# Turning the first half of h at an item's end, ahead of a run-time branch (sparse attention and expert MLP, one core)

## The chip, the core and the metric

The kernel runs on one core of one Trainium2 chip. The metric is device time in microseconds of the execution: the median of 3 runs.

## The reference

Local and global attention over 8 batches of 8 heads (512 local and 32 global positions, head size 64), and then a mixture of experts on the 4352 rows of 512 values that come out. Only the second part matters here:

```python
xn = x / (np.linalg.norm(x, axis=-1, keepdims=True) + 1e-06)
logits = xn @ en.T / tau
expert_idx = np.argmax(logits, axis=1)
for e in range(E):
    mask = expert_idx == e
    h = np.maximum(x[mask] @ w1[e], 0.0)
    out[mask] = gate_w[mask, None] * (h @ w2[e])
```

There are 8 experts; `w1[e]` is 512 x 1024 and `w2[e]` is 1024 x 512. How many rows an expert gets is known only at run time.

## The kernel before

The attention part writes its rows, sorted by expert, to a table in DRAM (`xs`). Then the expert part works in items of 128 rows of one expert. The number of items depends on the data: it lies between `NSURE` = 32 and `NI` = 48. Items 0 to 31 (`NSURE` - 1) are written out without a branch. Behind them stands a nest of run-time branches (`rest`, L1465): ahead of each further item every engine compares the item count with the item's number and either falls through into the next item or jumps to a closing block (`close`, L1424) that stands far behind. With the inputs here there are 36 items, 0 to 35: four branches fall through, and the fifth is taken.

Numbers are kept in two parts. A tensor is rounded to a high part by a ScalarE cast (`xH`, `hH`, `WH`), and VectorE subtracts that from the tensor to get the low part (`xL`, `hL`, `WL`). A product is then three TensorE products: high by high, high by low, low by high.

An item `w` does two steps, one item apart:

- up, for its own rows: `h = relu(x @ w1)`, in two halves of 512 columns. `up(0)` and `up(1)` are 12 products each. `send_h` (L1332) takes the relu on ScalarE and sends the half of h to DRAM (`hd`) from ScalarE's DMA queue; `get_h` (L1264) brings it back turned by blocks (`hq`) through SP's queue.
- down, for the item before (`pend`): `down(0)` and `down(1)` are 12 products each, 8 with `hH` and 4 with `hL`. Each needs its half of h to be turned on VectorE in blocks of 32 (`turn_h`, L1267, into `hk`) and rounded on ScalarE and VectorE (`split_h`, L1270). There is one `hk`, which both halves use in turn.

Beside this each item turns and splits the rows of the next item (`turn_x` into `xk`, `split_x`), and splits one staged half of an expert's weights, in eight chunks per item (`w_parts`, L1294: cast `WH` on ScalarE, subtraction `WL` on VectorE). An item's result is scaled and scattered by token two items later (`give`, L172: ScalarE `ob`, VectorE the token copy, POOL the scatter).

The order is written out by hand (`tc.manual_schedule()`): each engine runs its instructions in the order in which the code of `item` issues them, and waits by semaphores on the others. TensorE runs `up(0)`, `up(1)`, `down(0)`, `down(1)`. VectorE and ScalarE run, from item 3 on, the order of the last `else` of `item` (L1389 to L1409): turn of x, turn of the first half of h, split of x, one weight chunk, split of that half, turn of the second half, the first relu, and so on, and at the end the five last weight chunks. At an item's start each engine reads its entries of the item table into registers (`entry`, L1212): 

```python
        return eng.value_load(tab["tab"][w : w + 1, i : i + 1], min_val=0, max_val=top)
```

The closing block for item 35 is: turn and split of the first half, the result of item 34, `down(0)`, turn and split of the second half, `down(1)`, the result of item 35.

Of the kernel before, what the change touches and what calls it, by code (L numbers as in the profile page):

```python
# [98 lines left out]
def _sure_items(nt):  # L99
    return (nt - EARLY * P) // P  # L100
# [7 lines left out]
def tile_kernel(ctx: ExitStack, tc: tile.TileContext, qk, va, emb, tau, wraw, cst, out):  # L108
# [5 lines left out]
    NSURE = _sure_items(NT)  # L114
# [30 lines left out]
    def cols(st, lo, hi):  # L145

        r = lo // WRUN
        return st[:, r, lo - r * WRUN : hi - r * WRUN]
# [17 lines left out]
    def turn_blocks(xT, x):  # L166

        nc.vector.transpose(  # L168
            xT.rearrange("p (k t n) -> p t k n", k=4, t=4), x.rearrange("p (t k n) -> p t k n", t=4, k=4)
        )  # L170

    def give(gt, g2, ob):  # L172

        nc.scalar.activation(ob[:, :DM], g2, AF.Copy, scale=gt[:, 0:1])
        nc.vector.tensor_copy(ob[:, DM : DM + 1].bitcast(U32), gt[:, 1:2].bitcast(U32))
        nc.gpsimd.indirect_dma_start(  # L176
            out=out[:, :],
            out_offset=bass.IndirectOffsetOnAxis(ap=ob[:, DM : DM + 1].bitcast(U32), axis=0),
            in_=ob[:, :DM],
            in_offset=None,  # L180
            bounds_check=NT - 1,
            oob_is_err=False,
        )
# [1028 lines left out]
    def entry(eng, i, w, top):  # L1212

        if w < 2:
            return (EARLY * P + w * P, 2 + w, 0, 2 + w)[i]
        return eng.value_load(tab["tab"][w : w + 1, i : i + 1], min_val=0, max_val=top)

    def load_x(w):
        r = entry(nc.sync, 0, w, NE * CAP)
        return rows_of(xrs[w % 2], gts[w % 5], xs[ds(r, P), :], True)  # L1220
# [14 lines left out]
    def parts_of(tH, tL, x):  # L1235
        nc.scalar.copy(tH, x)  # L1236
        nc.vector.tensor_tensor(tL, x, tH, ALU.subtract)

    def flat(t):
        return t.rearrange("p c n -> p (c n)")  # L1240
# [12 lines left out]
    def relu(nh, g):  # L1253
        nc.scalar.activation(  # L1254
            hs[nh].rearrange("p (g k n) -> p k g n", g=4, k=4),
            g.rearrange("p (k g n) -> p k g n", k=4, g=4),
            AF.Relu,
        )

    def put_h(w, nh):  # L1260
        hd = hds[w % 2][nh].rearrange("p n -> (p n)").rearrange("(g p n) -> p g n", g=4, p=P)
        nc.scalar.dma_start(hd, hs[nh].rearrange("p (g n) -> p g n", g=4))

    def get_h(w, nh):  # L1264
        nc.sync.dma_start(hqs[nh], hds[w % 2][nh])

    def turn_h(nh):  # L1267
        turn_blocks(hk, hqs[nh])

    def split_h(nh):  # L1270
        ks = slice(4 * nh, 4 * nh + 4)
        parts_of(flat(hH[:, ks, :]), flat(hL[:, ks, :]), hk)

    def entries(w):
        return entry(nc.scalar, 3, w, 3), entry(nc.vector, 3, w, 3)

    def item(w, pend):

        xH, xL = xHs[w % 2], xLs[w % 2]
        rp = entry(nc.tensor, 2, w, 1)  # L1280
        regs = entries(w)
        if w < 2:
            held.append((w, regs))
        reads = []
        made = []
        todo = [(w, regs, c) for c in range(8)]
        if w == 0:
            todo = todo[:4]
        elif w == 1:
            todo = [(*held[0], c) for c in range(4, 8)] + [(*held[1], c) for c in range(4)]  # L1290
        elif w == 2:
            todo = [(*held[1], c) for c in range(4, 8)] + todo

        def w_parts(n):  # L1294
            for _ in range(min(n, len(todo))):
                v, (ra, rv), c = todo.pop(0)
                cs = slice(c * 512, (c + 1) * 512)
                s3 = cols(st0[v % 2], cs.start, cs.stop).unsqueeze(1)
                a = nc.scalar.copy(WH[c][:, ds(ra, 1)], s3)  # L1299
                b = nc.vector.tensor_tensor(WL[c][:, ds(rv, 1)], s3, WH[c][:, ds(rv, 1)], ALU.subtract)  # L1300
                made.extend([(v, c, a), (v, c, b)])

        def product(o, a, W, hf, start=False, stop=False):
            w3 = W[:, ds(rp, 1), hf * 512 : (hf + 1) * 512]
            return nc.tensor.matmul(o.unsqueeze(1), a, w3, start=start, stop=stop)  # L1305

        def up(nh):
            g = ps_1.tile([P, 512], F32, name="g1")
            for k in range(4):
                c = 2 * k + nh  # L1310
                reads.append(product(g, xH[:, k, :], WH2[c], 0, start=k == 0))
                reads.append(product(g, xH[:, k, :], WL2[c], 0))
                reads.append(product(g, xL[:, k, :], WH2[c], 0, stop=k == 3))
            return g

        out = {}

        def down(nh):
            if nh == 0:
                out["g2"] = g2s[w % 2]  # L1320
            g, ks, made = out["g2"], range(4 * nh, 4 * nh + 4), []
            for k in ks:
                made.append(product(g, hH[:, k, :], WH2[k], 1, start=k == 0))
                made.append(product(g, hH[:, k, :], WL2[k], 1))
            for k in ks:
                made.append(product(g, hL[:, k, :], WH2[k], 1, stop=k == 7))
            return made

        def done():
            give(gts[w % 5], out["g2"], obp.tile([P, DM + 1], F32, name="ob"))  # L1330

        def send_h(nh, g):  # L1332
            relu(nh, g)
            put_h(w, nh)

        ga = up(0)
        if "done" in pend:
            pend["done"]()
        if w > 2 and w + 1 < NI:
            load_w(w + 1)  # L1340
        if w + 2 < NI:
            load_x(w + 2)
        if w == 0:
            send_h(0, ga)
            w_parts(2)
            send_h(1, up(1))
            get_h(w, 0)
            first_w(1, 0, 1)
            get_h(w, 1)
            first_w(1, 1, 4)  # L1350
            w_parts(2)
        elif w == 1:
            w_parts(2)
            send_h(0, ga)
            w_parts(2)
            turn_h(0)
            split_h(0)
            gb = up(1)
            reads.extend(pend["down"](0))
            send_h(1, gb)  # L1360
            get_h(w, 0)
            load_w(w + 1)
            turn_h(1)
            split_h(1)
            turn_x(w + 1)
            split_x(w + 1)
            w_parts(4)
            get_h(w, 1)
            reads.extend(pend["down"](1))
        elif w == 2:  # L1370
            turn_x(w + 1)
            turn_h(0)
            split_x(w + 1)
            split_h(0)
            turn_h(1)
            send_h(0, ga)
            w_parts(2)
            split_h(1)
            gb = up(1)
            reads.extend(pend["down"](0))  # L1380
            send_h(1, gb)
            w_parts(2)
            get_h(w, 0)
            load_w(w + 1)
            w_parts(8)
            get_h(w, 1)
            reads.extend(pend["down"](1))
        else:
            if w < NI - 1:  # L1389
                turn_x(w + 1)  # L1390
            turn_h(0)
            if w < NI - 1:
                split_x(w + 1)
            w_parts(1)
            split_h(0)
            turn_h(1)
            send_h(0, ga)
            w_parts(1)
            split_h(1)
            w_parts(1)  # L1400
            gb = up(1)
            reads.extend(pend["down"](0))
            send_h(1, gb)
            get_h(w, 0)
            w_parts(8)
            get_h(w, 1)
            if w in (8, NSURE - 1):
                nc.gpsimd.drain()
            reads.extend(pend["down"](1))  # L1409
        for v, c, m in made:  # L1410
            for r in reads:
                tc.declare_no_dep(m.ins, r.ins, reason="the other slot")
                tc.declare_no_dep(r.ins, m.ins, reason="the other slot")
        for i, (v, c, m) in enumerate(made):
            for u, d, o in last_made + made[:i]:
                if c == d and (v - u) % 2:
                    tc.declare_no_dep(m.ins, o.ins, reason="another half")
        last_made[:] = made
        after = {"down": down, "next": done}
        if "next" in pend:  # L1420
            after["done"] = pend["next"]
        return after

    def close(pend):  # L1424
        turn_h(0)
        split_h(0)
        if "done" in pend:
            pend["done"]()
        pend["down"](0)
        turn_h(1)  # L1430
        split_h(1)
        pend["down"](1)
        pend["next"]()
# [123 lines left out]
```

## Time and profile before

| what | us |
|---|---|
| median of 3 runs | 693.06 |
| lowest and highest | 692.15, 702.01 |
| profiled execution | 689.4 |
| its span, first to last instruction | 687.5 |
| TensorE busy in the span | 627.8 (91%) |
| VectorE busy | 525.4 (76%) |
| ScalarE busy | 455.0 (66%) |

The profiled execution is one execution; its span leaves out the start and the end around the instructions.  The trace names engines PE (TensorE matmul), PEld (TensorE weight load), DVE (VectorE), ACT (ScalarE), POOL (GpSimd) and SP (SyncE); a "q" behind the name is the engine's sequencer, which handles register work, branches, semaphores and DMA issues, and L1300 is line 1300 of the kernel above. In brackets stands how long the engine was idle before an instruction and what ended that.

### The profile page before, as it was taken

The page shows a single profiled execution, that of the slowest core. Times are in us where ns is not written, and L with a number is a line of the kernel's source. Part 1 is how long each engine was busy: PE and PEld are TensorE (multiplying, and loading weights), DVE is VectorE, ACT ScalarE, POOL GpSimd, SP SyncE. Part 2 cuts the span into 40 slices and gives each one's busy share as a digit, 9 for nine tenths or more (in the row PEclk, how much of TensorE's full clock was granted, in tenths as well). Part 3 has the DMA queues.
Part 4 walks back from the last instruction along what each step waited for, and adds up shares of the span by engine and source line. Part 5 has one row for each costly group of instructions (what it writes and reads, how often), then busy time and mean ns, then how long its engine had stood idle before and what let it go on. Part 6 is the DMA issues. An engine that isn't in the chain of part 4 may idle for free.

```text
span 687.5 us, 23125 instructions
## 1 busy us (share of the span) xinstructions
PE 627.8 (91%) x7425; PEld 492.7 (72%) x7425; DVE 525.4 (76%) x1724; ACT 455.0 (66%) x962; POOL 94.9 (14%) x172
## 2 busy tenths in 40 slices
PE   9889788878888899779999999999999999999994
PEld 4667567666666546648888888888888877878873
DVE  2869777698887877668888888786888877878971
ACT  4777667657676436557777676766677766767761
POOL 2011221212313330001101001010101100110101
PEclk9999999999999999999999999999999999999997
DMA  9998889788898558767654586778877787876550
GB/s 276 321 274 265 253 260 278 211 272 284 280 329 274 158 167 243 245 206 233 192 161 145 150 261 207 202 211 287 239 229 220 222 256 231 229 227 171 147 158 23
DMA packets 125654, 154.66 MB, mean 225 GB/s; under 512 B 15945, under 2 KB 81609, under 8 KB 125528
## 3 DMA queue, kind: packets, MB, share of 16 engines
q1 hardware_dynamic: 81752, 116.32, 57.6%
q10 hardware_dynamic: 38016, 18.88, 9.2%
q0 software_dynamic: 5760, 17.87, 6.9%
q8 instruction: 69, 1.13, 0.7%
q14 instruction: 57, 0.47, 0.2%
HBM read 161.36 MB, written 40.94 MB: 294 GB/s over the span
## 4 chain that ended last, share of the span: by engine, by line
PE 68%; DMA 9%; DVE 8%; issue 8%; ACT 4%; SPq 1%; ACTq 1%; POOL 0%; DVEq 0%; another core or an unknown queue 0%; POOLq 0%
PE g L1305 45%; PE pt L199 7%; PE po L196 6%; PE pt L196 6%; PE s_ps L196 4%; DMA xr<-xs 2%; DMA hd<-h 2%; DMA raw<-in_qk_dram 2%; DMA hq<-hd 1%; ACT WH L1299 1%; DVE pb L536 1%; DMA xs<-xt,si 1%; DVE WL L1300 1%; DVE xt L598 1%; ACT pb L553 1%
## 5 line engine op out<-in xcount | busy, mean ns | idle before, releaser
L1300 DVE TENSOR_TENSOR WL<-stg,WH 128x512 f32 (+1 forms) x288 | 184.7, 684 | 37.3 <-ACT WH L1299 36.8
L1299 ACT CAST WH<-stg 128x512 f32 (+1 forms) x288 | 163.6, 618 | 37.1 <-ACT h L1254 36.0
L1305 PE MATMUL g<-WH,hH 128*128 (+1 forms) x288 | 114.6, 398 | 15.3 <-ACT hH L1236 15.3
L1305 PE MATMUL g<-WL,hH 128*128 (+1 forms) x288 | 113.6, 394 | 0.0
L1305 PE MATMUL g<-WL,xH 128*128 (+1 forms) x288 | 112.5, 391 | 0.9 <-DVE WL L1300 0.9
L1305 PE MATMUL g<-WH,xH 128*128 (+1 forms) x288 | 112.5, 391 | 0.0
L1305 PE MATMUL g<-WH,xL 128*128 (+1 forms) x288 | 112.1, 389 | 0.0
L176 POOL DMA_INDIRECT out_dram<-ob x37 | 36.0, 974 | 392.7 <-DVE xk L168 134.2
L553 ACT ACTIVATE pb<-pb,nm 128x128 f32<-128x128 f32 x256 | 80.1, 395 | 11.9 <-DVE nm L536 11.9
L1305 PE MATMUL g<-WH,hL 128*128 (+1 forms) x288 | 78.1, 394 | 0.0
L1305 PEld LDWEIGHTS g<-WH,hH 128*128 128x128 f32 x288 | 54.8, 190 | 30.4 <-ACT hH L1236 13.4
L168 DVE STREAM_TRANSPOSE hk<-hq 128x512 f32<-128x512 f32 x72 | 50.6, 703 | 22.4 <-DMA hq<-hd 17.0
L1305 PEld LDWEIGHTS g<-WL,xH 128*128 128x128 f32 x288 | 54.1, 188 | 14.0 <-DVE WL L1300 2.7
L1305 PEld LDWEIGHTS g<-WH,hL 128*128 128x128 f32 x288 | 55.0, 191 | 11.7
L1305 PEld LDWEIGHTS g<-WL,hH 128*128 128x128 f32 x288 | 54.9, 191 | 11.2
L1305 PEld LDWEIGHTS g<-WH,xH 128*128 128x128 f32 x288 | 54.1, 188 | 11.4 <-ACT xH L1236 0.2
L1305 PEld LDWEIGHTS g<-WH,xL 128*128 128x128 f32 x288 | 54.0, 188 | 11.1
L1236 ACT CAST hH<-hk 128x512 fp32r<-128x512 f32 x72 | 44.6, 619 | 22.3 <-DVE hk L168 21.9
L196 PE MATMUL s_ps<-raw 64*32 64x128 f32 (+1 forms) x1792 | 46.2, 280 | 11.4 <-issue 7.4
L536 DVE CUSTOM_DVE_ANT_0 pb<-s_ps,mask 128x128 f32<-128x128 f32 x192 | 44.2, 286 | 13.4 <-PE s_ps L196 13.4
L196 PE MATMUL po<-vt,pT 128*32 128x65 f32 x2048 | 41.7, 230 | 13.4 <-issue 12.9
L1236 ACT CAST xH<-xk 128x512 fp32r<-128x512 f32 x37 | 22.9, 619 | 45.3 <-DVE xk L168 45.2
(199 smaller groups left out, 885.1 us busy)
## 6 DMA issues: line engine op xcount, KB each, us to landing
stg<-in_wraw_dram SPq DMA_DIRECT2D x70, 1024.0 KB
vt<-in_va_dram SPq DMA_DIRECT2D x96, 260.0 KB
hd<-h ACTq DMA_DIRECT2D x72, 256.0 KB
hq<-hd SPq DMA_DIRECT2D x72, 256.0 KB
raw<-in_qk_dram SPq DMA_DIRECT2D x56, 304.0 KB
xr<-xs SPq DMA_DIRECT2D x152, 64.0 KB
vt<-in_va_dram SPq DMA_DIRECT2D x32, 130.0 KB
stg<-in_wraw_dram SPq DMA_DIRECT2D x16, 256.0 KB
```

The costliest lines, as they stand in the source:

```text
L168: nc.vector.transpose(xT.rearrange("p (k t n) -> p t k n", k=4, t=4), x.rearrange("p (t k n) -> p t k n", t=4, k=4))
L176: nc.gpsimd.indirect_dma_start(out=out[:, :], out_offset=bass.IndirectOffsetOnAxis(ap=ob[:, DM : DM + 1].bitcast(U32), axis=0), in_=ob[:, ...
L196: return counted(nc.tensor.matmul(out, lhsT, rhs, start=start, stop=stop), 4 if lhsT.dtype == F32 else 2)
L199: return counted(nc.tensor.transpose(out, in_, eye), 2)
L536: nc.vector.tensor_tensor_reduce(state["pb", g][grp][:, cs], ps[:, grp, cs], mk, -ISQ, 3.0e38, ALU.add, ALU.min, nm[:, n : n + 1],)
L553: nc.scalar.activation(pb[:, cs], pb[:, cs], AF.Exp, bias=nm[:, n : n + 1], scale=-1.0)
L598: nc.vector.tensor_tensor(x, p4[:, :, :, :D], rs.unsqueeze(3).to_broadcast([P, 2, 4, D]), ALU.mult)
L1236: nc.scalar.copy(tH, x)
L1299: a = nc.scalar.copy(WH[c][:, ds(ra, 1)], s3)
L1300: b = nc.vector.tensor_tensor(WL[c][:, ds(rv, 1)], s3, WH[c][:, ds(rv, 1)], ALU.subtract)
L1305: return nc.tensor.matmul(o.unsqueeze(1), a, w3, start=start, stop=stop)
```

## The change

For the items from `NSURE` - 1 = 31 on, turn and split of the first half of h are issued at the end of the same item, behind its fetch, and so ahead of the branch. Before, they were issued behind the branch, in the next item or in the closing block. In items 3 to 31 the turn at the item's start stays where it was. The amount of work is the same.

```diff
@@ -1388,11 +1388,13 @@
             if w < NI - 1:
                 turn_x(w + 1)
-            turn_h(0)
+            if w < NSURE:
+                turn_h(0)
             if w < NI - 1:
                 split_x(w + 1)
             w_parts(1)
-            split_h(0)
+            if w < NSURE:
+                split_h(0)
             turn_h(1)
             send_h(0, ga)
@@ -1406,7 +1408,11 @@
             get_h(w, 1)
             if w in (8, NSURE - 1):
                 nc.gpsimd.drain()
+            if w >= NSURE - 1:
+                turn_h(0)
             reads.extend(pend["down"](1))
+            if w >= NSURE - 1:
+                split_h(0)
@@ -1422,8 +1428,6 @@
     def close(pend):
-        turn_h(0)
-        split_h(0)
         if "done" in pend:
             pend["done"]()
         pend["down"](0)
```

On VectorE, at the end of item 32 and the start of item 33 (`hk<-hq_5776` is the turn of the first half, `hq_5777` the second, `xk` the turn of x, `tab` the table of the items):

```order
-L1471 COMPARE_AND_BRANCH
+L168 STREAM_TRANSPOSE hk<-hq_5776 128x4x4x32
+L1237 TENSOR_TENSOR hL<-hk,hH 128x512
+L1475 COMPARE_AND_BRANCH
 L1216 TENSOR_LOAD tab
 L1216 ISA x2
 L175 COPY ob<-gt_5771 128x1
 L168 STREAM_TRANSPOSE xk<-xr_5768 128x4x4x32
-L168 STREAM_TRANSPOSE hk<-hq_5776 128x4x4x32
 L1237 TENSOR_TENSOR xL_5783<-xk,xH_5781 128x512
 L1300 ISA
 L1300 TENSOR_TENSOR WL_5760<-stg_91,WH_5752 128x512
-L1237 TENSOR_TENSOR hL<-hk,hH 128x512
```

The turn and the subtraction stand one behind the other, ahead of the branch and of the table read; before, the turn stood between the turn of x and its subtraction, and `hL` behind the first weight chunk.

On ScalarE, at the same place (`WH` is the last weight cast of item 32, `hH` the cast of the first half of h):

```order
 L1299 COPY WH_5759<-stg_90 128x512
-L1471 COMPARE_AND_BRANCH
+L1236 CAST hH<-hk 128x512
+L1475 COMPARE_AND_BRANCH
 L1216 TENSOR_LOAD tab
 L1216 ISA x2
```

The cast moved from between the first weight cast of item 33 and its first relu to ahead of the branch.

On VectorE, in the closing block behind the taken branch (`gt` holds the gates and tokens of the item whose result is given out; the branch row ends the closing block that is written ahead of this one):

```order
-L1471 UNCONDITIONAL_BRANCH
-L168 STREAM_TRANSPOSE hk<-hq_5776 128x4x4x32
-L1237 TENSOR_TENSOR hL<-hk,hH 128x512
+L1475 UNCONDITIONAL_BRANCH
 L175 COPY ob<-gt_5770 128x1
 L168 STREAM_TRANSPOSE hk<-hq_5777 128x4x4x32
 L1237 TENSOR_TENSOR hL<-hk,hH 128x512
 L175 COPY ob<-gt_5771 128x1
```

The closing block begins with the token copy; the turn of the first half is no longer in it.

## Rows read from the trace of the kernel before

**Rows 1.** Busy time by stretch: engine busy us (instructions), granted clock, DMA.

```profile
628.00:669.20 41.20, 41.20 (x183) 34.11 (x182) 35.79 (x60) 30.52 (x55) 3.90 (x4) 1.00 0.54 149
```

**Rows 2.** Time line of VectorE, item 33: start, us, engine, line, operation.

```profile
638.25 0.70 DVE L168 STREAM_TRANSPOSE xk<-xr 128x512 f32<-128x512 f32 x1
638.88 0.67 DVE L168 STREAM_TRANSPOSE hk<-hq 128x512 f32<-128x512 f32 x1
...
640.85 0.68 DVE L1237 TENSOR_TENSOR hL<-hk,hH 128x512 fp32r<-128x512 f32 x1
641.57 0.71 DVE L168 STREAM_TRANSPOSE hk<-hq 128x512 f32<-128x512 f32 x1
...
645.14 3.10 DVE L1300 TENSOR_TENSOR WL<-stg,WH 128x512 f32 x5 [0.87 <-ACT WH L1299]
...
648.22 0.70 DVE L168 STREAM_TRANSPOSE xk<-xr 128x512 f32<-128x512 f32 x1
```

**Rows 3.** Time line of ScalarE, item 33.

```profile
638.98 0.62 ACT L1236 CAST xH<-xk 128x512 fp32r<-128x512 f32 x1 [1.18 <-DVE xk L168]
...
640.03 0.61 ACT L1236 CAST hH<-hk 128x512 fp32r<-128x512 f32 x1
640.55 0.59 ACT L1254 ACTIVATE h<-g 128x512 f32<-128x512 f32 x1
```

**Rows 4.** Time line, item 32: turns, second half's cast, its first product.

```profile
628.28 0.71 DVE L168 STREAM_TRANSPOSE xk<-xr 128x512 f32<-128x512 f32 x1
...
631.62 0.71 DVE L168 STREAM_TRANSPOSE hk<-hq 128x512 f32<-128x512 f32 x1
...
632.36 0.62 ACT L1236 CAST hH<-hk 128x512 fp32r<-128x512 f32 x1
...
634.15 0.39 PE L1305 MATMUL g<-WH,hH 128*128 x1
```

**Rows 5.** Sequencer of VectorE by line: ns min/median/max, first and last start.

```profile
L1471 DVEq COMPARE_BRANCH  x1: 43/43/43, 647.2 to 647.2; - x1
L1463 DVEq TENSOR_LOAD <-nitem x1: 309/309/309, 626.9 to 626.9; - x1
```

**Rows 6.** The taken branch ahead of the closing block, by sequencer.

```profile
L1471 PEldq COMPARE_BRANCH  x1: 3855/3855/3855, 665.4 to 665.4; - x1
L1471 DVEq COMPARE_BRANCH  x1: 67/67/67, 668.1 to 668.1; - x1
```

**Rows 7.** Chain that ended last, at the closing block: start, us, what.

```profile
673.13 0.05 DVEq L168
```

**Rows 8.** Time line of the end: last WL, products of both down steps, last scaling.

```profile
666.03 3.10 DVE L1300 TENSOR_TENSOR WL<-stg,WH 128x512 f32 x5 [0.82 <-ACT WH L1299]
...
666.79 0.39 PE L1305 MATMUL g<-WH,hH 128*128 x1
...
674.81 0.76 PE L1305 MATMUL g<-WH,hH 128*128 x1 [5.14 <-ACT hH L1236]
...
679.55 0.39 PE L1305 MATMUL g<-WH,hH 128*128 x1
...
682.47 0.69 ACT L174 ACTIVATE ob<-g,gt 128x512 f32<-128x512 f32 x1 [5.68 <-PE g L1305]
```

**Rows 9.** Busy time by stretch around two pauses; the clock stands behind POOL.

```profile
278.00:281.60 3.60, 0.16 (x1) 0.00 (x0) 2.31 (x4) 1.78 (x4) 0.00 (x0) 1.00 0.95 309
...
283.00:286.40 3.40, 3.40 (x10) 2.62 (x9) 2.03 (x5) 1.94 (x4) 0.00 (x0) 0.50 0.98 333
...
674.80:678.00 3.20, 3.19 (x8) 2.52 (x9) 2.09 (x5) 1.07 (x2) 0.97 (x1) 0.50 0.08 29
```

**Rows 10.** SP's queue: both fetches of h in items 33 and 35.

```profile
644.08 5.47 SPq L1265 DMA_DIRECT2D hq<-hd  x2
...
666.49 1.76 SPq L1265 DMA_DIRECT2D hq<-hd  x2
```

## The prediction

> **What bounds the kernel now.** I read the stretch in which the change acts, items 32 to 35 and what follows them, from about 628 us to the end of the span. First its engines by stretch: TensorE has no idle time at all between 628 and 669.2 us, at the full granted clock of 2.4 GHz, while VectorE is busy for 35.79 of the 41.20 us and ScalarE for 30.52 [rows 1]. So in the items the path is TensorE. One item takes it 10.88 us: the first product of the second half's down step stands at 634.15 in item 32 and at 666.79 in item 35, three items later [rows 4, 8]. Next the time line of VectorE and ScalarE over one item: VectorE goes from one `xk` turn to the next in 9.97 us (638.25 to 648.22) [rows 2], a little under TensorE's 10.88, so it keeps ahead. Last the end: TensorE sits idle for 5.14 us before the closing block, released by ScalarE's cast of `hH` [rows 8]. What the reader is to see is that VectorE and ScalarE have only 0.9 us to spare per item, and that the closing block is a chain of waits in which TensorE does two times 12 products.
>
> **How the order works before.** Inside an item VectorE runs the turn of x, then the turn of the old first half of h, and only then the rounding remainders. While ScalarE casts `xH`, VectorE does the turn of h [rows 2, 3]. Two dependent pairs are interleaved, and neither engine waits for the other.
>
> **Term 1: the moved instructions at an item's end.** Moved are one turn (0.71), one cast (about 0.62) and one subtraction (0.69) per item, for items 31 to 35; no DMA moves and nothing is added. At an item's end these three now stand alone, one waiting for the other: the turn follows the last `WL`, the cast can start only when the turn is done, the subtraction only after the cast. With a hand-over of 0.03 to 0.04 us (the turn of `xk` ends at 638.95, the cast of `xH` starts at 638.98 [rows 2, 3]) the subtraction starts 0.71 + 0.04 + 0.62 + 0.04 = 1.41 us after the last `WL` ended. Behind it stand the branch, the read of the table and the register work of the next item, which an engine's sequencer reaches only after the subtraction was let go. The branch at 647.2 is followed by the turn of `xk` at 648.22, 1.0 us later [rows 2, 5]. Today that 1.0 us is hidden below the last `WL`s (these end at 648.24, the turn starts at 648.22 [rows 2]). Afterwards it starts about 0.1 us after the subtraction starts, so the next turn of `xk` comes 1.41 + 0.1 + 1.0 = 2.5 us after the last `WL` instead of at once.
>
> What comes back inside the item: the subtraction no longer stands ahead of the turn of the second half (640.85 to 641.57, 0.72), and the cast no longer ahead of the relu (640.03 to 640.55, 0.52) [rows 2, 3]. The rest of the item hangs on the relu, the send and the second half's cast, so I count 0.65 of the two. Net 2.5 - 0.65 = 1.85 us per item on VectorE and ScalarE: 9.97 + 1.85 = 11.8 us, against 10.88 for TensorE. The two engines become the bound, and TensorE loses 0.9 us in each item once the slack is used.
>
> The slack is used in the first one. In item 32 the table's first read also stands there (the item count, 0.31 us, about 0.4 with its gaps [rows 5]); it is in both orders. The turn of `xk`, now at 628.28, moves 2.5 us; the turn of the second half at 631.62 moves 2.5 - 0.72 = 1.8 us, its cast from 632.36 to 634.1, ready at 634.75. TensorE starts that product at 634.15 and loads its weights 0.23 us before [rows 4]. It waits 0.6 to 0.8 us; I take 0.7. Items 33 to 35 add 0.9 each. Together 0.7 + 2.7 = 3.4 us: TensorE is through item 35 at 669.67 + 3.4 = 673.1 (669.67 is 674.81 less the idle 5.14 [rows 8]).
>
> Bounds of this term: from 0 (if the register work overlaps the wait as it overlaps the `WL`s today and the slack suffices) to 4 x 1.85 = 7.4 us. I take 3.4, which is what the rows of one item give.
>
> **Term 2: the closing block.** Here the change is to help. TensorE's own sequencer took the branch at 665.4 and was through it 3.86 us later, at 669.3, ahead of the array [rows 6], so its code is there. VectorE took its branch at 668.1, and its next entry stands at 673.13, 5.0 us later [rows 6, 7]: that is what delayed the first turn. Afterwards the turn does not wait for it. But VectorE's branch then stands behind the subtraction, and the 5.0 us start later. Item 35's turn of `xk` is at 628.28 + 2.5 + 3 x 11.8 = 666.2; its last `WL` ends 10.0 - 0.65 = 9.35 later at 675.5 (today 666.03 + 3.10 = 669.1 [rows 8]); turn and cast end at 676.9, so TensorE's first closing product is at 677.0, not 674.81. VectorE's branch is at 677.1, its closing code at 682.1, the copy of the token and the second half's turn end at 683.0, the cast at 683.7. The second 12 products start there, not at 679.55 [rows 8]: +4.1 us. That already holds the 3.4 of term 1. The rest behind it (12 products, 2.9 us to ScalarE's 682.47, then the scatter) is as before.
>
> A branch itself costs 0.067 us in VectorE's row [rows 6]; the 5.0 us are the wait for the code behind it. The Trainium skill (Advanced Engine Details and Errata, Control Flow Timing) gives about 108 ns for a compare-and-branch. By that alone the second half's turn would follow at once, the 12 products would wait only for the first 12, and the change would come out within 0.5 us of before. The trace disagrees for a taken branch: 5.0 us on VectorE here.
>
> **Term 3: TensorE's clock.** Today the pause of 5.14 us ends with the granted clock at 0.50, 1.2 GHz, from 674.8 to 678 [rows 9], and the first 12 products take 679.55 - 674.81 = 4.7 us, against 2.9 for the second 12 at 2.4 GHz [rows 8]. Afterwards there are two pauses, 673.1 to 677.0 and about 680 to 683.7. If the clock is low in the first 12, nothing is lost, since the second 12 wait for VectorE anyway. If it is low in the second 12, it costs 4.7 - 2.9 = 1.8 us. The nearest row: TensorE had next to no work from 278.0 to 281.6, and stood at 0.50 from 283.0 to 286.4, after it had resumed [rows 9]. Bounds 0 and 1.8; I take 1.0.
>
> **Cost taken as nothing.** The turn needs `hq`, whose fetch SP issued at 666.49 for item 35 and at 644.08 for item 33 [rows 10], before the last `WL`s in both. Relu and sends move later with ScalarE, and the fetch with them, so it stays just ahead. If that cover went, each item would lose what the fetch is late, some 0 to 2 us.
>
> **Sum.** 4.1 + 1.0 = +5.1 us on the profiled execution, 689.4 to 694.5 us (span 687.5 to 692.6). The median of the runs shown, 693.06, lies 3.7 above the profiled execution, and the lowest is 692.15; I set the level of a timed run at 692.6 and forecast 697.7 us. That is 0.7% slower, well below the 2% (13.9 us) which is about what a measurement of this kernel can tell from no change.
>
> **Rivals.**
> Faster: VectorE's register work runs while the subtraction waits, so its items stay under 10.88 and TensorE loses nothing. Then the last `WL` ends at 669.1, TensorE resumes at 670.6 after a pause of 1 us at 2.4 GHz, and VectorE's code comes at 675.6, the second 12 start at 677.3: 2.2 us gained, 690.4. For it speaks that the register work overlaps now; against it that it stands behind a waiting instruction on an in-order engine. It decides at item 32: the cast of `hH` must be ready by 633.9.
> No difference: the items lose about half as much as I say and the closing block gives it back. 692 to 694.5. For it speaks the 5.14 us pause, the largest idle time there; against it the 5.0 us behind VectorE's branch, which only move.
> Worse: fetched h comes late at the head of VectorE's queue. In item 33 the second fetch ended 5.5 us after the first was issued [rows 10]; 2 us in three items, with both closing blocks at 1.2 GHz, make 697.7 + 6 = 704.
>
> **How the numbers follow.** Forecast 0.60 (own range 695 to 700.5), no difference 0.17, faster 0.13, worse 0.10. The range 690.5 to 702.5 reaches to the faster case and part of the worse one. All cases but the far end of the worse one are within 13.9 us: faster by over 2% 0.01, within 2% 0.96, slower by over 2% 0.03.
>
> **What would show it.** Right: between 628 and 673 TensorE has idle time of 0.6 to 1 us before the second half's down step in each of items 32 to 35, ended by ScalarE's `hH`; the `xk` turns stand 11.6 to 12 us apart; the closing block's second 12 products wait about 4 us for `hH`. Wrong: TensorE stays without idle time to 669, or the second half's turn in the closing block comes no later than 675.4. The forecast falls if the `xk` turns stand under 10.9 us apart.

## The result and the profile after

The changed kernel took 697.57 us (median of 8 runs, 695.52 to 701.39), beside it the kernel before 692.70 us (8 runs, 691.08 to 702.01): a ratio of 1.0072, with a 95% interval of 1.0043 to 1.0101. A later pair on another chip gave 694.6 against 690.9 us, a ratio of 1.0051 (1.0009 to 1.0093). It is slower by 3.5 to 4.9 us, well inside 2%. In some executions the whole kernel runs one or two per cent slower; the medians here are of all executions, the ratios leave those out.

Two profiled executions differ by more than the change: the first product of item 32 stands at 629.54 us in the changed kernel and at 625.96 before, though hardly anything ahead of it was touched. So lengths are counted here from that product on. The table shows the two executions first compared, and a second one of each kernel (runs a2 and b2 below).

| from item 32's first product, us | before | changed | before again | changed again | step forecast |
|---|---|---|---|---|---|
| to the end of item 35's last product | 43.7 | 48.3 | 43.7 | 47.0 | +3.4 |
| TensorE's pause ahead of the closing block | 5.1 | 3.7 | 3.5 | 3.7 | -1.2 |
| first 12 closing products, until the second 12 start | 4.7 | 5.3 | 4.4 | 4.4 | +2.0 |
| second 12 | 2.9 | 2.9 | 2.9 | 3.0 | +1.0 |
| sum | 56.5 | 60.2 | 54.5 | 58.1 | +5.1 |

The forecast's steps stand in its own terms: 673.1 less 669.67; a pause from 673.1 to 677.0; 677.0 to 683.7 for the first 12; the clock (each rounded). Measured is +3.7 (60.2 less 56.5) and +3.6 (58.1 less 54.5).

The changed kernel by stretch (columns as in [rows 1]):

```profile
628.00:669.20 41.20, 38.55 (x167) 30.45 (x166) 31.16 (x51) 26.04 (x48) 2.92 (x3) 1.00 0.49 138
...
681.50:686.80 5.30, 5.23 (x12) 4.12 (x13) 2.14 (x5) 1.31 (x2) 0.97 (x1) 0.50 0.07 20
686.80:690.00 3.20, 2.96 (x13) 2.09 (x11) 0.04 (x1) 0.21 (x1) 0.00 (x0) 0.99 0.23 87
```

In the stretch in which TensorE had no idle time [rows 1] it now has 2.65 us of it, the first three of the four waits below (with the later start of this execution, the stretch now ends inside item 35). VectorE and ScalarE did less work there (31.16 against 35.79, 26.04 against 30.52): they are not fuller, they wait.

What TensorE waited for from 629 to 678 us, in the view of waits (us in total, times, longest):

```profile
PE g L1305 <- ACT hH L1236: 3.1, 4, 1.3
```

Two of these four waits, and the pause ahead of the closing block, on TensorE's time line:

```profile
637.14 0.84 PE L1305 MATMUL g<-WH,hL 128*128 x3
638.92 0.50 PE L1305 MATMUL g<-WH,hH 128*128 x1 [0.94 <-ACT hH L1236]
639.26 0.40 PE L1305 MATMUL g<-WL,hH 128*128 x1
...
674.81 0.50 PE L1305 MATMUL g<-WH,hH 128*128 x1 [0.50 <-ACT hH L1236]
...
676.76 1.08 PE L1305 MATMUL g<-WH,hL 128*128 x4
681.57 0.76 PE L1305 MATMUL g<-WH,hH 128*128 x1 [3.73 <-ACT hH L1236]
...
686.83 0.42 PE L1305 MATMUL g<-WH,hH 128*128 x1
```

There is one wait in each of items 32 to 35, always ahead of the second half's down step, as forecast: 0.94, 0.43, 1.28, 0.50. In the closing block only the first 12 products are waited for. The 24 need one pause, not two.

VectorE at the end of item 31, around the end of item 32 and the start of item 33, and at the end of item 33, where the moved work stands:

```profile
631.98 0.71 DVE L168 STREAM_TRANSPOSE hk<-hq 128x512 f32<-128x512 f32 x1 [0.43 <-DMA hq<-hd]
...
641.06 3.10 DVE L1300 TENSOR_TENSOR WL<-stg,WH 128x512 f32 x5 [0.78 <-ACT WH L1299]
644.07 0.70 DVE L168 STREAM_TRANSPOSE hk<-hq 128x512 f32<-128x512 f32 x1
645.52 0.69 DVE L1237 TENSOR_TENSOR hL<-hk,hH 128x512 fp32r<-128x512 f32 x1 [0.74 <-ACT hH L1236]
646.28 0.15 DVE L175 COPY ob<-gt 128x1 uint32<-128x1 uint32 x1
646.49 0.71 DVE L168 STREAM_TRANSPOSE xk<-xr 128x512 f32<-128x512 f32 x1
647.89 0.69 DVE L1237 TENSOR_TENSOR xL<-xk,xH 128x512 fp32r<-128x512 f32 x1 [0.69 <-ACT xH L1236]
...
656.55 0.71 DVE L168 STREAM_TRANSPOSE hk<-hq 128x512 f32<-128x512 f32 x1 [0.74 <-DMA hq<-hd]
...
658.98 0.71 DVE L168 STREAM_TRANSPOSE xk<-xr 128x512 f32<-128x512 f32 x1
```

Here the loss of an item can be read. In [rows 2] the last `WL` ends at 648.24 and the next `xk` starts at 648.22. Here the last `WL` ends at 644.16 (641.06 + 3.10) and `xk` follows at 646.49, 2.33 us later. In between VectorE turns, waits 0.74 us for ScalarE's cast, subtracts, and goes through the register work. The pair for x now stands alone as well (0.69 us idle for `xH`): the turn of h that used to fill this gap [rows 2] is gone. And the moved turn is now the first to feel a late fetch: it waited 0.43 us at 631.98 (item 31) and 0.74 us at 656.55 (item 33). In the repeated run of the changed kernel (a2 below) no moved turn waited for its fetch.

The closing block on VectorE:

```profile
679.97 0.70 DVE L168 STREAM_TRANSPOSE hk<-hq 128x512 f32<-128x512 f32 x1
681.42 0.69 DVE L1237 TENSOR_TENSOR hL<-hk,hH 128x512 fp32r<-128x512 f32 x1 [0.74 <-ACT hH L1236]
684.58 0.15 DVE L175 COPY ob<-gt 128x1 uint32<-128x1 uint32 x1 [2.47 <-issue]
684.69 0.71 DVE L168 STREAM_TRANSPOSE hk<-hq 128x512 f32<-128x512 f32 x1
```

and the taken branch, by sequencer (ns; first and last start):

```profile
L1475 PEldq COMPARE_BRANCH  x1: 4867/4867/4867, 676.4 to 676.4; - x1
...
L1475 DVEq COMPARE_BRANCH  x1: 67/67/67, 681.4 to 681.4; - x1
```

The turn of the first half no longer waits for code, as intended. The wait for code moved behind the subtraction, from the branch at 681.43 to the copy at 684.58: 3.1 us, where [rows 6, 7] gave 5.0. It lies beside the first 12 products, which end later than the second half's cast is done (the turn at 684.69, then 0.7 and 0.6 us, some 686.05, against 686.83), so it costs nothing. In the repeated run the margin is only 0.1 us (684.05 against 684.13).

### The profile page after: what moved, and what is told of

Read it like the earlier page. It is cut to its first block, busy times and chain, and to the rows that moved or that the text cites. A ratio compares the mean times of both kernels' runs of the same rounds, so it can differ in the third digit from the quotient of the medians.

```text
span 695.7 us, 23120 instructions
## 1 busy us (share of the span) xinstructions
PE 631.3 (91%) x7423; PEld 491.6 (71%) x7425; DVE 525.8 (76%) x1724; ACT 455.7 (66%) x962; POOL 94.8 (14%) x172
## 4 chain that ended last, share of the span: by engine, by line
PE 45%; DMA 16%; DVE 14%; issue 12%; ACT 7%; SPq 3%; ACTq 1%; DVEq 1%; POOL 0%; POOLq 0%; another core or an unknown queue 0%
PE g L1305 24%; PE pt L199 6%; PE po L196 6%; DMA hq<-hd 5%; PE pt L196 5%; DMA hd<-h 5%; PE s_ps L196 4%; DVE WL L1300 3%; ACT WH L1299 3%; DMA raw<-in_qk_dram 3%; DMA xr<-xs 2%; ACT h L1254 2%; DVE hk L168 1%; DVE xk L168 1%; DVE pb L536 1%
## 5 line engine op out<-in xcount | busy, mean ns | idle before, releaser
L168 DVE STREAM_TRANSPOSE hk<-hq 128x512 f32<-128x512 f32 x72 | 50.7, 704 | 24.9 <-DMA hq<-hd 23.9
L196 PE MATMUL s_ps<-raw 64*32 64x128 f32 (+1 forms) x1792 | 47.5, 278 | 14.6 <-issue 10.7
L196 PE MATMUL po<-vt,pT 128*32 128x65 f32 x2048 | 46.0, 231 | 13.6 <-issue 12.6
L565 ACT COPY pT<-pt 128x512 f32<-128x512 f32 x64 | 34.4, 588 | 33.1 <-PE pt L199 32.7
```

The source lines that it names most:

```text
L168: nc.vector.transpose(xT.rearrange("p (k t n) -> p t k n", k=4, t=4), x.rearrange("p (t k n) -> p t k n", t=4, k=4))
L196: return counted(nc.tensor.matmul(out, lhsT, rhs, start=start, stop=stop), 4 if lhsT.dtype == F32 else 2)
L565: nc.scalar.copy(pT, state["tp", g, grp])
```

## The experiments

The theory, called S in the expectations: the moved turn, cast and subtraction stand in series at the item's end with the register work behind them, VectorE's and ScalarE's item grows to some 11.7 us, and TensorE (10.88 us) starves. The rivals: the branch and the code behind it set the loss, or the executions merely differ. One slip stands on record: where an expectation counts the 56.5 us of the kernel before from item 33, it is counted from the first product of item 32, as in the table above; so are all tails below. Medians and ratios are against the kernel before on the same chip; "items" are the lengths of items 32, 33 and 34 on TensorE.

### Is it the branch? The same order in all items from 3 on

Items 3 to 31 have no branch.

```diff
-            if w < NSURE:
+            if w < 4:
                 turn_h(0)
...
-            if w >= NSURE - 1:
+            if w >= 3:
                 turn_h(0)
```

(the same two conditions at `split_h`)

> The new order not from item 31 but from item 3 on, so also in 28 items that have no branch behind them. Theory S: the same 0.8 us is lost in each of these 28 items too, +20 to +27 us over the changed kernel, 715 to 724; turns of x 11.5 to 11.9 us apart all along. Rival B: items without a branch lose nothing, 696 to 700. Rival U (the 4.9 us are drift between executions, not the items): 692 to 698.

Measured: 724.2 us, ratio 1.0469 (1.0394 to 1.0544). TensorE's item is 11.65 us in the median of items 4 to 31, against 10.88 before. VectorE over one item of it, then what was waited for from 400 to 640 us:

```profile
450.89 0.71 DVE L168 STREAM_TRANSPOSE xk<-xr 128x512 f32<-128x512 f32 x1
...
461.58 0.69 DVE L1237 TENSOR_TENSOR hL<-hk,hH 128x512 fp32r<-128x512 f32 x1 [0.74 <-ACT hH L1236]
...
462.48 0.71 DVE L168 STREAM_TRANSPOSE xk<-xr 128x512 f32<-128x512 f32 x1
```

```profile
PE g L1305 <- ACT hH L1236: 15.3, 17, 2.0
...
DVE hk L168 <- DMA hq<-hd: 10.5, 7, 2.6
```

From `xk` to `xk` are 11.59 us without any branch, so the branch isn't needed for the loss: 32 us in all, at the far edge of the 715 to 724 us that S expects. This repeats the effect some 30 times. The second row shows a part that S leaves out: 6 of 20 moved turns waited for their fetch (the seventh wait is a turn of a second half).

### The register work: read ahead of the turn

As the run before, but the next item's table entries are read ahead of the moved turn, where `WL`s are still queued.

```diff
-        regs = entries(w)
+        regs = pend["regs"] if "regs" in pend else entries(w)
...
+            if 3 <= w < NI - 1:
+                ahead.append(entries(w + 1))
             if w >= 3:
                 turn_h(0)
```

> As the run with the new order in all items, but VectorE and ScalarE read the next item's table entry (two register reads) ahead of the turn of the first half, not behind the subtraction. Theory S (1.85 us more per item on VectorE: 1.4 of it waiting one behind the other, 0.36 the register reads that stick out behind the subtraction): 0.36 us less in each of 32 items, 11 us less than that run, 710 to 716 beside 724.2; turns of x 11.3 to 11.5 us apart. Rival B (the whole price is the register work behind a waiting instruction): 692 to 698. Rival W (only the wait): 722 to 726.

Measured: 715.52 us, ratio 1.0383 (1.0322 to 1.0444). That is 25.0 us above the kernel before on its chip, where the run before was 32.2 us above it on another; the intervals of the two ratios overlap, so the rows have to show the size. Its profiled execution took 723.1 us, so only neighbouring rows are read in it:

```profile
453.46 0.69 DVE L1237 TENSOR_TENSOR hL<-hk,hH 128x512 fp32r<-128x512 f32 x1 [0.74 <-ACT hH L1236]
454.07 0.14 DVE L175 COPY ob<-gt 128x1 uint32<-128x1 uint32 x1
454.13 0.70 DVE L168 STREAM_TRANSPOSE xk<-xr 128x512 f32<-128x512 f32 x1
```

From the subtraction's start to `xk` are 0.67 us, against 0.90 in the run before (461.58 to 462.48) and 0.97 in the changed kernel. So the register work behind the waiting subtraction sticks out by 0.2 to 0.3 us per item; the rest of the loss is the serial work itself and, in some items, the late fetch.

### The serial work without the move

The kernel before, with turn and split of the first half in series at the item's start, behind the branch; once from item 32 on, once from item 4 on.

```diff
+            if w >= NSURE:
+                turn_h(0)
+                split_h(0)
             if w < NI - 1:
                 turn_x(w + 1)
-            turn_h(0)
+            if w < NSURE:
+                turn_h(0)
```

> Of the kernel before: in items 32 to 47 turn, cast and subtraction stand one behind the other at the item's start, behind the branch and ahead of the turn of x; the closing block is as before. Theory S: VectorE's item is 9.97 + 1.5 = 11.5 us, TensorE loses 0.5 us in each of four items, +1.5 to 2.5 us, 694 to 695.5; in the profile the turns of x stand 11.3 to 11.6 us apart. Rival B (it is the branch and the register reads behind the waiting subtraction that cost): the same as before, 692 to 693, turns of x 10.9 apart.

> Of the kernel before: in items 4 to 47 turn, cast and subtraction stand one behind the other at the item's start, behind the register reads and ahead of the turn of x. Nothing is ahead of a branch. Theory S: 11.3 us per item as in the run with this in items 32 to 35 alone, so 0.43 us lost in each of 32 items, 705 to 711. Rival B: 691 to 695.

Measured: from item 32 on 695.18 us, ratio 1.0022 (0.9978 to 1.0067), which doesn't tell it from before; its items are 10.88, 11.14, 11.29 and its tail 58.7. From item 4 on 717.94, ratio 1.0437 (1.0377 to 1.0496), 7 us above the highest figure expected, with 11.55 us per TensorE item. VectorE in the short one:

```profile
651.41 0.70 DVE L168 STREAM_TRANSPOSE hk<-hq 128x512 f32<-128x512 f32 x1
652.80 0.69 DVE L1237 TENSOR_TENSOR hL<-hk,hH 128x512 fp32r<-128x512 f32 x1 [0.69 <-ACT hH L1236]
653.41 0.71 DVE L168 STREAM_TRANSPOSE xk<-xr 128x512 f32<-128x512 f32 x1
...
662.72 0.70 DVE L168 STREAM_TRANSPOSE hk<-hq 128x512 f32<-128x512 f32 x1
```

An item takes 11.31 us (651.41 to 662.72), as expected. The miss of the long one was mine: I took 0.43 us per item from the short run for all items. Seven of items 6 to 14 of the long run do take TensorE 11.26 to 11.38 us; later ones take up to 13.8, and the median of 11.55 means 0.67 lost. With the slack gone, waits that the old order hid may count in full there; they were not taken apart. So the series by itself, with no move, loses nearly as much (27 us) as the changed order in all items (32 us).

### The turn alone

The turn at the item's end, the split at its old place; from item 31 on, and from item 3 on.

```diff
             w_parts(1)
-            if w < NSURE:
-                split_h(0)
+            split_h(0)
...
             reads.extend(pend["down"](1))
-            if w >= NSURE - 1:
-                split_h(0)
...
     def close(pend):
+        split_h(0)
```

> Of the changed kernel, only the turn of the first half of h stays ahead of the branch; its cast and subtraction stand again between the first weight chunk and the second half's turn, and in the closing block at its start. Theory S (the turn, the cast and the subtraction stand alone one behind the other, and that makes VectorE's item longer than TensorE's 10.88 us): VectorE pays only the turn, 9.97 + 0.71 = 10.7 us per item, TensorE has no idle time in items 32 to 35, and in the closing block the first 12 products start about 2 us earlier than in the kernel before (VectorE need not turn there), so 1 to 4 us faster than before, 689 to 692 beside 692.7. Rival B (the price comes from having VectorE wait for the fetched h and then branch later): TensorE still waits 0.5 to 1 us in each item, time 694 to 698.

> Only the turn of the first half at an item's end, in all items from 3 on; cast and subtraction stay at their old place in the next item. Theory S: VectorE's item is 10.7 us, below TensorE's 10.88, nothing is lost but the fetch that now and then comes late at the head of VectorE's queue: 691 to 697. Rival B (VectorE waiting for the fetched h at the end of every item): 710 or more.

Measured: 695.44 us, ratio 1.0047 (0.9998 to 1.0097), not the gain S expected; its tail is 56.3, as before, with items of 11.35, 10.88, 11.14. From item 3 on: 712.46, ratio 1.0292 (1.0218 to 1.0366), where S expected 691 to 697; the rival's figure of 710 or more came out. By these times alone the rival would have it. The trace of the long one says where they come from. TensorE in its items 8 to 14, and in the same seven items of the run with the series at the start (columns as in [rows 1]):

```profile
368.20:444.30 76.10, 76.10 (x337) 63.06 (x336) 63.35 (x106) 54.30 (x99) 6.80 (x7) 1.00 0.67 198
```

```profile
368.80:448.60 79.80, 78.19 (x337) 62.44 (x336) 62.34 (x106) 53.76 (x99) 6.81 (x7) 1.00 0.64 193
```

With the turn alone TensorE has no idle time in these items and takes 10.88 us for each, as in the kernel before; VectorE's turns of x stand 10.55 us apart in three of them, near S's 10.7. The same items take TensorE 11.42 us each in the mean with the series at the start, and 11.73 with the changed order in all items. So where h comes in time (the longest wait for it in these items of the turn alone is 0.63 us) the turn alone costs nothing, the series costs 0.5 us and the changed order 0.85 us per item.

The 22 us of the turn alone arise in the other items. VectorE's waits for h in that run from 330 to 690 us:

```profile
DVE hk L168 <- DMA hq<-hd: 26.6, 19, 3.6
```

The way of h can be followed in item 33 of the changed kernel, where the turn at 656.55 waited 0.74 us (from the chain that ends at that turn: start, us, what):

```profile
648.90 3.37 DMA hd<-h
...
652.34 4.12 DMA hq<-hd
```

The send takes 3.37 us and the fetch 4.12, until 656.46, while the last `WL` had ended at 655.82 (652.72 + 3.10). With the turn at the end of VectorE's item a loop closes: the turn of x, up, relu, the send of h, its fetch, the turn of h, and only then the next turn of x. So S explains what each item of the changed kernel loses, but it isn't the only limit: with the series away, the move still loses wherever the fetch of h is late. What makes it late in some items and not in others was not tried.

### The turn earlier, between the weights

Turn behind the third of the last five weight chunks, cast and subtraction behind the fourth and fifth, so that other work fills the gaps.

```diff
+            if w >= NSURE - 1:
+                w_parts(3)
+                turn_h(0)
+                w_parts(1)
+                split_h(0)
             w_parts(8)
```

(the two statements behind the fetch go)

> Of the changed kernel, turn, cast and subtraction of the first half still stand ahead of the branch, but spread among the last five weight chunks: three chunks, turn, one chunk, cast and subtraction, one chunk. Theory S: the cast runs beside a weight chunk and the register reads run below the last one, VectorE's item is about 10.7 us, no idle time of TensorE in the items except where the fetched h is not there yet (item 34, up to 1 us); the closing block starts without the 5.1 us pause: 2 to 5 us faster than before, 688 to 691. Rival B (the branch comes later, the closing code later): like the change, 695 to 698.

Measured: 693.85 us, ratio 0.9999 (0.9961 to 1.0037): no gain over before. Two of the turn's waits:

```profile
652.26 0.71 DVE L168 STREAM_TRANSPOSE hk<-hq 128x512 f32<-128x512 f32 x1 [0.76 <-DMA hq<-hd]
...
675.98 0.71 DVE L168 STREAM_TRANSPOSE hk<-hq 128x512 f32<-128x512 f32 x1 [1.26 <-DMA hq<-hd]
```

The turn now waits for the fetch (0.76, 0.23, 1.26 us in items 33 to 35), VectorE stands still, and the items are 11.86, 11.39, 11.92. This is the same wait that the turn alone showed.

### What the closing block alone gives

The move for item 35 alone (its number written into the code, so it fits this data only), and, the other way round, the kernel before with the branch early: the last five weight chunks go behind the branch, and are dropped in the closing block, which doesn't use them.

```diff
-            if w < NSURE:
+            if w != LAST + 1:
                 turn_h(0)
...
-            if w >= NSURE - 1:
+            if w == LAST:
                 turn_h(0)
```

```diff
+        if "late" in pend:
+            pend["late"]()
...
-            w_parts(8)
+            if w < NSURE - 1:
+                w_parts(8)
```

> The move for item 35 alone, which is the last one with these inputs (its number is written into the code); items 32 to 35 keep the old order at their start, so no item loses anything. What is left is the closing block. Theory S, with what the first runs showed (the fetched h of the last item lands about 1 to 2.5 us after TensorE is through): TensorE's pause falls from 5.1 to 1.5 to 3.9 us, the code behind VectorE's branch comes 3 to 5 us after the subtraction and sets the second 12 products: 0 to 3 us faster than before, from TensorE's start of item 33 to its end 53.5 to 56.5 us beside 56.5. Rival C (the closing block gains what the 5.1 us pause is worth): 4 us or more faster.

> Of the kernel before: from item 31 on the last five weight chunks of an item are split behind the branch, at the next item's start, ahead of its first products in the order, and not at all in the closing block, where nothing reads them. Turn, cast and subtraction stand where they stood before. Theory S: the items lose nothing (the order on VectorE and ScalarE is the same, only the branch and the register reads move into VectorE's wait for the cast); VectorE's branch comes about 3 us earlier than its last weight chunk, its closing code at about 670, and the first half is turned as soon as its fetch has landed: TensorE's pause 1.3 to 3 us instead of 5.1, no second pause, from TensorE's start of item 33 to its end 51 to 54 us beside 56.5 before; 2 to 5 us faster, 686 to 690. Rival C (the pause is the fetch of h, not the code): pause 4 us or more, no gain.

Measured: the move for item 35 alone took 687.77 us, ratio 0.9978 (0.9943 to 1.0013); its tail is 52.9. The early branch took 691.54, ratio 0.9984 (0.9936 to 1.0033); its tail is 53.1 and its items 10.88 each. Both tails are as forecast or a little better, 1.4 to 3.6 us below the two of the kernel before (54.5, 56.5), but neither total can be told from before; that of the early branch missed its 686 to 690. TensorE in the move for item 35, and its clock in the two halves of the closing block (columns as in [rows 1]):

```profile
675.35 0.47 PE L1306 MATMUL g<-WH,hH 128*128 x1 [1.64 <-ACT hH L1237]
...
679.79 0.50 PE L1306 MATMUL g<-WH,hH 128*128 x1 [1.45 <-ACT hH L1237]
```

```profile
675.30:678.30 3.00, 2.95 (x12) 2.22 (x12) 0.66 (x2) 0.69 (x1) 0.00 (x0) 1.00 0.04 11
679.80:682.90 3.10, 3.04 (x12) 2.16 (x12) 0.72 (x2) 0.02 (x1) 0.39 (x1) 1.00 0.22 85
```

Two short pauses, both halves at the full 2.4 GHz. So by the tail of its one profile the move helps the closing block, where nothing follows it; the timed runs do not show the gain. In the changed kernel VectorE arrives late: its moved turn starts at 679.97, 2.1 us after TensorE was through (677.84).

With the early branch the closing turn waited for its fetch:

```profile
674.95 0.71 DVE L168 STREAM_TRANSPOSE hk<-hq 128x512 f32<-128x512 f32 x1 [4.61 <-DMA hq<-hd]
```

That fetch was issued at 671.26 and landed 3.56 us later, at 674.82. So what is left of TensorE's pause there (2.08 us) is the way of h, not the code.

### Both kernels again

> The changed kernel once more, for a second profile: from TensorE's start of item 33 to its end 59 to 62 us as in the first (60.2), with waits of 0.4 to 1.3 us for the cast of h in each of items 32 to 35. If the first profile's 3.7 us were drift (rival U): 55 to 58 us. Time 3 to 7 us above the kernel before.

> The kernel before once more, for a second profile: from TensorE's start of item 33 to its end 56 to 58 us as in the first (56.5). If rival U holds, it scatters as far as the changed kernel's. Ratio to itself within 0.3% of 1.

Measured: changed 694.6 us, ratio 1.0051 (1.0009 to 1.0093), tail 58.1, a little under what was expected. Before 689.45, ratio 0.9986 (0.9946 to 1.0025), tail 54.5, also under it. In the changed kernel, two of VectorE's turns of x and TensorE's pause; then the start of the closing block in the one before:

```profile
645.54 0.71 DVE L168 STREAM_TRANSPOSE xk<-xr 128x512 f32<-128x512 f32 x1
...
657.21 0.71 DVE L168 STREAM_TRANSPOSE xk<-xr 128x512 f32<-128x512 f32 x1
...
679.71 0.47 PE L1305 MATMUL g<-WH,hH 128*128 x1 [3.69 <-ACT hH L1236]
```

```profile
672.03 0.71 DVE L168 STREAM_TRANSPOSE hk<-hq 128x512 f32<-128x512 f32 x1 [2.48 <-SPq L1471]
...
673.61 0.47 PE L1305 MATMUL g<-WH,hH 128*128 x1 [3.53 <-ACT hH L1236]
```

VectorE's 11.67 us per item comes again: the turns of x stand 11.89, 11.67 and 11.69 us apart here, 11.66, 12.49 and 11.73 in the first execution. The later end of item 35 in the first one (48.3 against 47.0) lies in items 32 and 34 (12.23 and 12.55 us on TensorE, against 11.59 and 11.67), each behind a turn that waited for its fetch. What differs between the two of the kernel before is the time from VectorE's branch to its next entry, 3.4 us here and 5.0 in [rows 6, 7], and with it the pause, 3.53 us here and 5.14 in [rows 8]. The profile puts the end of that wait down to SP, whose own entries behind the branch start at 671.5; whether VectorE's code or SP came last, the trace does not settle. The 5.0 us on which a term of the forecast stood was one draw of a quantity that scatters.

## Why the prediction was right, and where it was not

**The whole.** +5.1 us forecast, +4.9 and +3.7 measured in the medians (697.57 less 692.70, 694.6 less 690.9), +3.7 and +3.6 in the tail. 697.7 us was forecast, 697.57 measured. Term 1 was right in mechanism and nearly in size; the right total also owes something to errors of opposite sign in the others.

**Term 1, the serial work at an item's end: right.** By its steps: 2.5 us from the last `WL` to the next `xk` (2.33 measured), 0.65 given back inside the item (9.99 us from `xk` to the end of the last `WL` in [rows 2], and 644.16 less the `xk` at 634.83, 9.33, afterwards: 0.66), so 11.8 us per item on VectorE (11.66 to 11.89 measured, 12.49 in the one item whose fetch was late). The idle times of 0.94, 0.43, 1.28 and 0.50 add up to 3.15 us, 3.4 forecast; in the repeated run 1.86 (0.32, 0.64, 0.42, 0.48). That the branch isn't needed was shown by the order in all items; that the series is enough, by the series without the move; and that without it an item whose h comes in time loses nothing, by items 8 to 14 of the turn alone.

What the term left out: a wait costs more than its idle figure. TensorE was through with item 35 4.6 us later (3.3 in the repeated run), against idle times of 3.15 (1.86), some 0.36 us more per wait. The rows show 0.27 of it: a product's modelled end lies 0.39 us behind its start, while the next starts after 0.23, so 0.16 of the gap isn't called idle; and behind a wait the second product follows after 0.34 (638.92 to 639.26) instead of 0.23. The rest I could not place.

**"Cost taken as nothing", the fetch: too low.** "It stays just ahead" held in three of the five moved turns; those of items 31 and 33 waited 0.43 and 0.74 us for `hq`, and items 32 and 34 behind them were the longest on TensorE (12.23 and 12.55). The step that failed took the issue of a fetch for its arrival: in item 33 the fetch was issued at 652.34, before the last `WL`s ended, and landed 4.12 us later, behind them. The 5.47 us of [rows 10] are no landing either, as the rival "worse" reads them: they run from the issue of the first fetch to that of the second, at 649.21. The run with the turn alone in all items shows what this term can cost, 22 us without any series.

**Term 2, the closing block: half right.** The first closing product was forecast 51.0 us behind item 32's first (677.0 less 625.96); it came after 52.0 and 50.7. VectorE's branch did go behind the subtraction. The step that failed is "the 5.0 us start later ... the second 12 products start there": the code came after 3.1 us (2.9 in the repeated run), and the first 12 products ran long enough at 1.2 GHz to cover it. No second pause exists. The second 12 start 3.7 us later than before (57.3 us behind item 32's first product, against 53.6), near the +4.1 forecast, but held by TensorE's own first 12 and not by `hH`; the repeated pair has +3.5 (55.1 against 51.6).

The Trainium skill (Advanced Engine Details and Errata, Control Flow Timing) has about 108 ns for a compare-and-branch. The row of VectorE's branch agrees in its order of size (67 ns), but 3.1 us pass until the engine's next instruction. A reason that fits is told in another place of the Trainium skill (Runtime: NRT & Kernel Launch, Instruction fetch mechanics): a taken branch to code outside of what is prefetched stalls until that code is fetched. It gives no size there; the runs here have 2.9 to 5.0 us on VectorE, and none of them shows the fetch of code itself.

**Term 3, the clock: wrong.** "If the clock is low in the first 12, nothing is lost, since the second 12 wait for VectorE anyway" failed with the second pause: the first 12 were at 0.50 and took 5.26 us, and the second 12 at 0.99 followed on their heels. Against before, whose first 12 were low as well, that is +0.5 us in the one pair and nothing in the other, where 1.0 was forecast.

**The rivals.** "Faster" falls: VectorE's register work did not run while the subtraction waited (0.97 us from the subtraction's start to `xk`; 0.67 where the reads were ahead). "No difference" (up to 694.5, 0.27% above before) is out by the interval of the first pair (0.43% at least); that of the second alone (0.09% at least) would not rule it out. Of "worse" a part is true, the late fetch, in two items of the first profile and in none of the second.

## What to carry to other kernels

An operation pair over two engines that is moved out of an interleaved place into one where it stands alone costs its own length and each hand-over; whether that matters is decided by the slack per item (here 0.9 us), and the register reads queued behind a waiting instruction come on top. A move that helps the last item only should be made for the last item only; in the loop it is paid in each. And before a limit is taken away, look for the one that stands close behind it: here a late fetch of h, which cost 22 us with the turn alone moved in all items, though nothing was lost where h came in time.

A wait for code behind a taken branch is a sample, not a constant; with single executions that drift by several us, compare lengths within the profile, from a fixed instruction on.

## What the runs showed of the hardware

**The wait for code scatters.** From VectorE's taken branch to its next instruction it took 5.0 us before, 3.4 in the repeated run, 3.1 and 2.9 in the changed kernel, 3.0 with the turn alone and with the move for item 35. (With the early branch it took 5.3 us, but there the fetch of h landed last.) TensorE's own branch (4.87 us, at 676.4) starts while the array still has work. In the changed kernel it ended at 681.27, only 0.3 us ahead of the first closing product: a little longer, and it would have been the bound. What sets the scatter was not tried.

**The length of a pause alone does not decide the clock.** After 1.64 and 1.45 us (the move for item 35) TensorE stayed at 2.4 GHz; after 2.08 us (the early branch) most of the next 12 products went at the lower level. But after nearly the same pause the fall came at different places: after 3.65 us (the turn between the weights) the products were 0.43 us apart or more from the first on; after 3.69 (the repeated changed kernel) only from the fifth on, and after 3.37 (the turn alone from item 3 on) from the seventh on. The first closing product with the turn between the weights:

```profile
677.54 0.77 PE L1305 MATMUL g<-WH,hH 128*128 x1 [3.65 <-ACT hH L1236]
```

The early branch, at the first closing product and by stretch:

```profile
676.53 0.47 PE L1305 MATMUL g<-WH,hH 128*128 x1 [2.08 <-ACT hH L1236]
```

```profile
676.40:681.00 4.60, 4.47 (x13) 3.63 (x14) 2.19 (x5) 1.19 (x2) 0.97 (x1) 0.63 0.16 59
681.00:684.50 3.50, 2.86 (x13) 2.01 (x11) 0.00 (x0) 0.60 (x1) 0.00 (x0) 1.00 0.02 5
```

The clock did not fall at once there: the products start 0.31 and 0.23 us apart at first (676.53, 676.84, 677.07), and some 0.43 us apart from 677.7 on; 0.63 is the mean over the stretch, 1.00 follows in the next.
